# A fourth output buffer, and final DMA waits moved in front of the last store, in a fused dilated-window attention and GEGLU kernel

## Chip, cores, metric

One core of a Trainium2 chip. The metric is the device time of one launch in microseconds (us), the median of several runs. Runs agree within about 0.5%, and this case is about tenths of a microsecond in 195, so most of the argument rests on traces, which resolve 0.01 us.

## The reference

Two branches on the layer-normed input, and a residual; 2048 rows of 512, bf16.

```python
def _A_ref(x, wqkv, wo):            # 32 heads of 16; window of 8 keys, 2 apart
    qkv = (x @ wqkv) ...
    kg = k[:, :, idx_c, :]...; vg = v[:, :, idx_c, :]...
    logits = einsum("bhsd,bhswd->bhsw", q, kg) * scale   # masked before position 0
    return einsum("bhsw,bhswd->bhsd", softmax(logits), vg)... @ wo
def _B_ref(x, w_gate, w_up, w_down):
    return (gelu(x @ w_gate) * (x @ w_up)) @ w_down      # 1376 hidden columns
xn = _layernorm(x)
return x + _A_ref(xn, A_wqkv, A_wo) + _B_ref(xn, B_w_gate, B_w_up, B_w_down)
```

## The kernel before

The program builds a graph of tasks and orders it with a list scheduler at build time; each engine then runs its list, and semaphores carry the dependencies. Buffers are slots of pools: a task that starts a new tile takes the slot that came free first, and then depends on everything that used it. The output is made in 19 pieces. TensorE sums attention output and down projection in PSUM, VectorE adds the residual XR into an output buffer OB, and SyncE stores it. The last 256 rows are cut into 256- and 128-column pieces to shorten the end.

```python
TAIL_SPLIT = {14: [(0, 256), (256, 512)], 15: [(0, 256), (256, 384), (384, 512)]}
NOB = cfg.get("NOB", 3)                       # output buffers
P_ob = Pool("ob", NOB)
junk = sb("junk", [128, 512], BF)             # scratch: the sums of one tile want an output
# ... per piece:
it_ob = Item("ob" + sfx, P_ob, "ob")
#   fin (VectorE):  OB[:, slot, 0:CW] = PS[...] + XR[:, slot, c0:c1]
#   sto (SyncE):    dma_start(out2[rows, c0:c1], OB[:, slot, 0:CW])
```

Every DMA task gets one of 24 semaphores in turn. A task's waits stand in front of it, and SyncE ends with a wait for the full count of all 24:

```python
def emit_engine(self, eng_name, e):
    ...
    for t in self.order[eng_name]:
        for (s, v) in t.waits:
            e.wait_ge(s, v)
        ins = t.emit(e)
        ins.then_inc(t.sem, 16 if eng_name == "sp" else 1)
    if eng_name == "sp":
        for (s, tot) in self.dma_totals:      # 24 of them
            e.wait_ge(s, tot)
```

## Time and profile before

| | us |
|---|---|
| time, median of the first 3 runs | 194.91 (194.59 to 194.97) |
| span of the profiled execution | 192.8 |
| last matmul ends (modelled) | 190.32 |
| last add (VectorE) | 190.44 to 190.73 |
| last store issued | 190.76 |
| last store landed | 192.21 |
| SyncE's branch to the end | 192.39 |

The first half of such a reading is where the span is bound (TensorE, 97%); the second is the **tail**, from the end of the last matmul to SyncE's branch: 192.39 - 190.32 = 2.07 us here. As long as the build-time order stays as it is, a change of buffers and final waits can act nowhere else. The prediction below shows the lines. In them PE, DVE, ACT, POOL and SP are TensorE, VectorE, ScalarE, GpSimd and SyncE, PEld is TensorE's weight load, and a q behind an engine marks its instruction sequencer; numbers in front are start and duration in us, and brackets give the idle time before an instruction and who ended it. A store is issued by a SyncE instruction and has landed, or is home, when its data is written and its semaphore counted; a wait is met when its semaphore already has the value.

### The profile page before, as it was taken

What the parts mean: (1) busy time and instruction counts of PE and PEld (TensorE: products, weight loads), DVE (VectorE), ACT (ScalarE), POOL (GpSimd) and SP (SyncE); (2) the same over time, 40 slices, a digit from 0 to 9 for tenths busy, and PEclk for the clock granted to TensorE, in tenths of its full rate; (3) what the DMA queues carried; (4) which work ended last, traced back from release to release, by engine and by line L of the source; (5) the groups of instructions that cost most, each with busy time, mean ns of one, the idle gap of its engine ahead of it and who ended that gap; (6) DMA issues with size and microseconds to landing.
All of it is one profiled execution on the core that took longest, in us unless ns stands there. A gap on an engine that the chain in (4) does not pass through costs nothing.

```text
span 192.8 us, 3283 instructions
## 1 busy us (share of the span) xinstructions
PE 186.6 (97%) x1239; PEld 92.0 (48%) x1256; DVE 152.4 (79%) x240; ACT 106.1 (55%) x177; POOL 15.7 (8%) x31
## 2 busy tenths in 40 slices
PE   6899999999999999999999999999999999999994
PEld 2794444444444444444444444444444444444484
DVE  5799999999997965999995599998996199912132
ACT  5688565696896766712466587328276720058000
POOL 7010011110931020000000000000000000000000
PEclk9999999999999999999999999999999999999999
DMA  4999997899564014965401596420250496130121
GB/s 143 353 397 332 307 172 139 229 235 219 146 131 106 0 40 134 239 140 161 146 19 28 143 237 157 130 77 0 69 139 13 113 233 165 36 112 0 51 72 46
DMA packets 34800, 27.04 MB, mean 140 GB/s; under 512 B 11264, under 2 KB 33248, under 8 KB 34784
## 3 DMA queue, kind: packets, MB, share of 16 engines
q1 hardware_dynamic: 34784, 26.83, 56.2%
q8 instruction: 10, 0.16, 0.3%
q14 instruction: 6, 0.05, 0.1%
HBM read 19.99 MB, written 5.26 MB: 131 GB/s over the span
## 4 chain that ended last, share of the span: by engine, by line
PE 93%; DMA 4%; issue 1%; SPq 0%; DVE 0%; DVEq 0%
PE PS L1395 36%; PE PS L1474 18%; PE PS L1152 18%; PE PS L1470 7%; PE PS L1098 4%; PE PS L1363 4%; PE PS L1236 4%; DMA Wqkv<-in_A_wqkv_dram 2%; PE PS L1430 2%; DMA out_dram<-OB 1%; PE PS L1229 1%; SPq L923 0%; DVE OB L1494 0%; PE PS L1040 0%; DVEq L558 0%
## 5 line engine op out<-in xcount | busy, mean ns | idle before, releaser
L1412 ACT ACTIVATE UU<-PS 128x512 bf16<-128x512 f32 x40 | 24.1, 603 | 35.7 <-PE PS L1395 35.7
L1474 PE MATMUL PS<-Wd,HT 128*128 128x512 bf16 (+2 forms) x207 | 41.1, 345 | 0.1
L1395 PE MATMUL PS<-xnT,Wu 128*128 128x512 bf16 x155 | 39.8, 379 | 0.7 <-issue 0.5
L1395 PE MATMUL PS<-xnT,Wg 128*128 128x512 bf16 x155 | 39.2, 379 | 0.5 <-ACT OT L1375 0.2
L1206 DVE TENSOR_TENSOR UNI<-QT,KT 128x2048 bf16<-128x2048 bf16 x32 | 37.0, 1219 | 2.6 <-PE PS L1363 2.5
L1152 PE MATMUL PS<-xnT,Wqkv 128*128 128x512 bf16 x156 | 35.3, 379 | 0.2
L1417 DVE TENSOR_TENSOR HT<-GG,UU 128x512 bf16<-128x512 bf16 x40 | 16.6, 419 | 20.1 <-ACT UU L1412 20.0
L1405 ACT ACTIVATE GG<-PS 128x512 bf16<-128x512 f32 x40 | 23.7, 601 | 15.0 <-PE PS L1395 12.2
L1474 PEld LDWEIGHTS PS<-Wd,HT 128*128 128x128 bf16 x209 | 19.6, 98 | 18.6
L1395 PEld LDWEIGHTS PS<-xnT,Wu 128*128 128x128 bf16 x160 | 15.3, 98 | 19.6 <-issue 1.3
L1395 PEld LDWEIGHTS PS<-xnT,Wg 128*128 128x128 bf16 x160 | 15.5, 98 | 19.3 <-ACT OT L1375 0.4
L1152 PEld LDWEIGHTS PS<-xnT,Wqkv 128*128 128x128 bf16 x160 | 15.6, 98 | 18.6
L1343 DVE TENSOR_TENSOR BS<-BS,PT 128x2048 bf16<-128x2048 bf16 x16 | 19.6, 1224 | 0.4
L1343 DVE TENSOR_TENSOR UNI<-BS,PT 128x2048 bf16<-128x2048 bf16 x16 | 19.5, 1218 | 0.0
L1494 DVE TENSOR_TENSOR OB<-PS,XR 128x512 bf16<-128x512 f32 (+2 forms) x19 | 11.2, 603 | 10.0 <-PE PS L1474 9.4
L1470 PE MATMUL PS<-Wo,OT 128*128 128x512 bf16 (+2 forms) x76 | 16.9, 345 | 0.0
L1176 ACT ACTIVATE VT<-PS 128x512 bf16<-128x512 f32 x16 | 9.6, 597 | 4.4 <-PE PS L1152 4.4
L1375 ACT ACTIVATE OT<-PS 128x512 bf16<-128x512 f32 x16 | 8.3, 602 | 5.0 <-PE PS L1363 5.0
L940 DVE BATCH_NORM_STATS2 st<-XIN 128x6 f32<-128x512 bf16 x15 | 10.1, 686 | 0.9 <-DMA XIN<-in_A_x_dram 0.9
L1470 PEld LDWEIGHTS PS<-Wo,OT 128*128 128x128 bf16 x76 | 7.2, 98 | 7.0
L1192 POOL COPY KT<-KT 128x64 bf16<-128x64 bf16 x3 | 8.0, 2655 | 17.5 <-ACT KT L1169 16.1
L1162 ACT ACTIVATE QT<-PS 128x512 bf16<-128x512 f32 x12 | 7.2, 597 | 3.1 <-PE PS L1152 3.1
(73 smaller groups left out, 151.9 us busy)
## 6 DMA issues: line engine op xcount, KB each, us to landing
BS<-vt_scratch SPq DMA_DIRECT2D x64, 128.5 KB, 3.5
vt_scratch<-VT SPq DMA_DIRECT2D x16, 128.0 KB
XR<-in_A_x_dram SPq DMA_DIRECT2D x16, 128.0 KB, 2.2
out_dram<-OB SPq DMA_DIRECT2D x14, 128.0 KB, 1.9
Wqkv<-in_A_wqkv_dram SPq DMA_DIRECT2D x3, 512.0 KB
XIN<-in_A_x_dram SPq DMA_DIRECT2D x6, 256.0 KB, 4.4
Wg<-in_B_w_gate_dram SPq DMA_DIRECT2D x1, 1280.0 KB
Wu<-in_B_w_up_dram SPq DMA_DIRECT2D x1, 1280.0 KB
```

Of the source, the lines that this page charges most:

```text
L940: return lambda e: e.bn_stats(out=st[:, t, :], in_=XIN[:, it.slot, t2, :])
L1152: ins = e.matmul(PS[:, 512 * it.slot:512 * it.slot + HWD], lhsT=lhsT, rhs=xnT[:, itx.slot, kt, c0:c0 + HWD], start=(kt == 0), stop=(kt == 3))
L1176: return lambda e: e.activation(out=VT[:, ito.slot, 0:HWD], in_=PS[:, 512 * it.slot:512 * it.slot + HWD], func=ACTF.Identity)
L1206: return lambda e: e.tensor_tensor(out=UNI[:, it.slot, :, :], in0=bass.AP(QT, (itq.slot * 4 + g) * 512, [[NQT * 4 * 512, 128], [0, 4], [1, ...
L1343: return lambda e: e.tensor_tensor(out=dst(), in0=bass.AP(BS, it.slot * 4 * 514 + o, [[NBS * 4 * 514, 128], [514, 4], [128, 4], [1, 128]]) ...
L1395: ins = e.matmul(PS[0:M, 512 * it.slot:512 * it.slot + 512], lhsT=Wx[:, kt, j * 128:j * 128 + M], rhs=xnT[:, itx.slot, kt, :], start=(kt = ...
L1405: return lambda e: e.activation(out=GG[0:M, ito.slot, :], in_=PS[0:M, 512 * it.slot:512 * it.slot + 512], func=ACTF.Gelu_apprx_tanh)
L1412: return lambda e: e.activation(out=UU[0:M, ito.slot, :], in_=PS[0:M, 512 * it.slot:512 * it.slot + 512], func=ACTF.Identity)
L1417: return lambda e: e.tensor_tensor(out=HT[0:M, ito.slot, j, :], in0=GG[0:M, ig.slot, :], in1=UU[0:M, iu.slot, :], op=ALU.mult)
L1470: ins = e.matmul(PS[:, 512 * it.slot:512 * it.slot + CW], lhsT=OT[:, ito.slot, dq, ti * 128:(ti + 1) * 128], rhs=Wo[:, dq, c0:c1], start=( ...
L1474: ins = e.matmul(PS[:, 512 * it.slot:512 * it.slot + CW], lhsT=HT[:, ith.slot, j, ti * 128:(ti + 1) * 128], rhs=Wd[:, j, c0:c1], start=Fal ...
L1494: return lambda e: e.tensor_tensor(out=OB[:, ito.slot, 0:CW], in0=PS[:, 512 * it.slot:512 * it.slot + CW], in1=XR[:, itx.slot, c0:c1], op= ...
```

## The change

The intent: the last add should not wait for a buffer that an earlier store still reads (fourth buffer; its kilobyte per partition comes from the scratch tile, whose job XR's first buffer takes while it is still unused), and SyncE should not work through 24 waits at the very end, when 19 of them were met long before.

```diff
             for (s, v) in t.waits:
                 e.wait_ge(s, v)
+            if eng_name == "sp" and t is self.order["sp"][-1]:
+                late = self.order["sp"][-5:]
+                for (s, tot) in self.dma_totals:
+                    if not any(q.sem is s for q in late):
+                        e.wait_ge(s, tot)
             ins = t.emit(e)
@@
         if eng_name == "sp":
-            for (s, tot) in self.dma_totals:
-                e.wait_ge(s, tot)
+            for q in self.order["sp"][-5:]:
+                e.wait_ge(q.sem, q.val)
@@
-    NOB = cfg.get("NOB", 3)
+    NOB = cfg.get("NOB", 4)
@@
-        junk = sb("junk", [128, 512], BF)
@@
-  ("sx1",  ... dict(out=junk[:, :],  func=ACTF.Identity, accum_out=sums[:, 0:1]), ...
+  ("sx1",  ... dict(out=XR[:, 0, :], func=ACTF.Identity, accum_out=sums[:, 0:1]), ...
-  ("sxx1", ... dict(out=junk[:, :],  func=ACTF.Square, bias=sums[:, 1:2], ...
+  ("sxx1", ... dict(out=XR[:, 0, :], func=ACTF.Square, bias=sums[:, 1:2], ...
```

More of the change, by code (lines that the diff above doesn't have):

```diff
@@ L942, in bass_parallel_sum__sliding_local_dilated__glu_gated_geglu__prompt_kernel @@
                     for (nm, dur, kw, rd, wr) in (
-                            ("sx1", 0.55, dict(out=junk[:, :], func=ACTF.Identity, accum_out=sums[:, 0:1]),
+                            ("sx1", 0.55, dict(out=XR[:, 0, :], func=ACTF.Identity, accum_out=sums[:, 0:1]),
                              [], [I_junk, (I_sums, 0)]),
@@ L946, in bass_parallel_sum__sliding_local_dilated__glu_gated_geglu__prompt_kernel @@
                                                 scale=-1.0 / D), [(I_sums, 0)], [(I_sums, 1)]),
-                            ("sxx1", 0.55, dict(out=junk[:, :], func=ACTF.Square, bias=sums[:, 1:2],
+                            ("sxx1", 0.55, dict(out=XR[:, 0, :], func=ACTF.Square, bias=sums[:, 1:2],
                                                 accum_out=sums[:, 2:3]), [(I_sums, 1)], [I_junk, (I_sums, 2)]),
```

## The prediction

> **What bounds the kernel now.** I read the page first: busy time by engine, then the chain that ended last. TensorE is busy 97% of the span at full clock, and the chain runs through it for 93% of the span. Whatever does not shorten TensorE's stream can only act in the tail behind its last matmul, where the chain goes to the output adds (L1494) and the stores of OB (L1501).
>
> ```profile
> PE 186.6 (97%) x1239; PEld 92.0 (48%) x1256; DVE 152.4 (79%) x240; ACT 106.1 (55%) x177; POOL 15.7 (8%) x31
> PE 93%; DMA 4%; issue 1%; SPq 0%; DVE 0%; DVEq 0%
> ```
>
> The waits view restricted to tile OB says who holds the 19 output adds: TensorE nearly always, a store that still owns its buffer once. That once is the last add.
>
> ```profile
>   PE PS L1474: 9.4, 7
>   DMA out_dram<-OB: 0.6, 1
> DMA to landing us min/median/max: 1.7/2.0/2.9
> ```
>
> The chain of waits in order of time shows it: with three buffers the nineteenth add takes the buffer of the sixteenth, whose store was issued at 187.56, landed 2.85 us later (the slowest of all; the median is 2.0), and released the last add at 190.44.
>
> ```profile
> 187.11 0.44 DVE OB L1494
> 187.56 2.85 DMA out_dram<-OB
> 190.41 0.02 issue
> 190.44 0.29 DVE OB L1494
> ```
>
> So 0.56 us of idle time is booked on the missing buffer. The timeline of the same stretch shows whether the add could have started earlier.
>
> ```profile
> 188.70 0.78 PE L1474 MATMUL PS<-Wd,HT 128*128 128x128 bf16 x11
> 189.54 0.78 PE L1474 MATMUL PS<-Wd,HT 128*128 128x128 bf16 x11
> 189.59 0.29 DVE L1494 TENSOR_TENSOR OB<-PS,XR 128x128 bf16<-128x128 f32 x1 [0.38 <-PE PS L1474]
> 190.44 0.29 DVE L1494 TENSOR_TENSOR OB<-PS,XR 128x128 bf16<-128x128 f32 x1 [0.56 <-DMA out_dram<-OB]
> ```
>
> The next-to-last piece's matmuls end at 188.70 + 0.78 = 189.48 and its add, released by TensorE, starts at 189.59: 0.11 us later. The four adds before it start 0.11 to 0.14 us after theirs (same timeline, same subtraction). The last matmuls end at 189.54 + 0.78 = 190.32, so the last add would start at 190.43 to 190.46 with a free buffer; it did start at 190.44. **Matmul and store release it together.** The wait is real but hides nothing.
>
> Behind the last add: the timeline of the DMA issues has the last store issued at 190.76, and the semaphore instructions of the final waits (L564) follow it.
>
> ```profile
> L564 SPq EVENT_SEMAPHORE  x12: 17/28/539, 191.1 to 192.3; - x12
> ```
>
> In windows of 0.01 us the twelve start 0.06 us apart (191.20, 191.27, 191.33, ... 191.69). The tenth lasts 539 ns, until 192.23: it is the one that waits for the last store. Two follow, at 192.27 and 192.33, then the branch to the end at 192.39. The first nine lie under the store's flight and cost nothing.
>
> **What the Trainium skill says.** Perfetto Trace Analysis, Identifying Dependency Chains: an instruction with several waits may have EventSemaphore instructions inserted ahead of it. The trace agrees: 24 final waits are 12 such instructions (two waits each, the first single, one wait on the branch). Advanced Engine Details and Errata, Network/Comms: reading a semaphore from a sequencer takes 50 to 100 ns; here the pitch is 60 ns for an instruction with two waits. DMA: Bandwidth & Descriptors, Anatomy of one DMA: some 2 us of fixed cost, mostly the receipt of the write (stated there for the GpSimd path); the stores here take 1.7 to 2.9 us from SyncE, and that is the term that neither part of this change touches. Perfetto Trace Analysis, Optimization Strategy: a bubble that repeats can mean too few buffers. On OB it does not repeat: one in nineteen.
>
> **The change part by part.**
>
> Fourth buffer. The last add now takes the buffer of the fifteenth, whose store went out at about 185.96 and at the slowest landing of 2.9 us is home by 188.9, 1.5 us before it is wanted. Gain: 190.44 minus 190.43, so 0.00 to 0.02 us. Nowhere else does an add wait for a store, so nothing before the tail moves.
>
> Scratch. The two ScalarE sums write 128x512 into XR's first buffer and not into their own tile: same instructions, 631 and 722 ns, same order. The first load of XR is issued at 33.2 us, long after the sums (about 5 us), and ScalarE's later work already stands in front of it. 0.00 us.
>
> Order of instructions. The order on each engine is fixed at build time by a list scheduler that counts OB buffers, so a fourth one could reorder everything. I went through the plan of the kernel before: of 19 adds only the fourth was planned to wait for its buffer (by some half a microsecond), and VectorE has planned slack behind it; the visible effect should be that one store changes place with one XR load near 94 us. No planned time enters the forecast. 0.00 us expected.
>
> Final waits. 24 waits become 19 in front of the last store and 5 behind it. In the kernel before as compiled, the first-emitted of several waits sits on the instruction itself and the others go into semaphore instructions ahead of it. For the last store the first-emitted is the wait for the last add, so the 19 others become 10 semaphore instructions ahead of that wait, in time where SyncE idles. How much idle time? The store before is issued at 189.89 and takes 0.33, until 190.23; the last add is done at 190.44 + 0.29 = 190.73. Idle: 0.50 us. Needed: from the end of a store issue to the first semaphore instruction 0.055, nine pitches of 0.06, and 0.06 to what follows: 0.655 us. The last store is issued at 190.23 + 0.655 = 190.88 rather than 190.76: **0.12 us lost**. Its flight (190.76 to 192.23, 1.47 us) is the same. All 19 are met by then; the youngest is an earlier tile's store.
> After the landing, the five last waits are two semaphore instructions and the branch; by the same rule the last store's wait sits in the second of them, so only the branch follows. Two instructions of 0.06 us fall away behind the landing: **0.12 us gained**.
> Sum: -0.01 +0.00 +0.12 -0.12 = -0.01 us, nothing. Since SyncE is now later than the last add, even the buffer's 0.01 is covered. 194.91 - 0.01 = 194.9.
>
> **Rivals.** (1) The buffer's 0.56 us counts in full, as the waits view books it: 194.4. Against it: the matmul's end plus the usual lag falls on the same moment. For it: matmul ends are modelled, and in executions where the reused store lands later the buffer protects; then part of it appears. (2) The 10 semaphore instructions stand behind the wait for the add, as the source text orders them: 0.6 lost and 0.12 gained, 195.4. Against it: every several-wait instruction of the kernel before is compiled the other way round. (3) They are fully hidden, because the sequencer runs them faster than in the tail of before: only the 0.12 is left, 194.8. (4) The build-time order drifts after all: plus or minus 1 us, as TensorE's stream has gaps of about 6 us in total that could grow or shrink; no direction.
>
> **Range and chances.** The three runs before spread by 0.38 us, more than any tail term alone. Rivals 1 and 2 set the ends at 194.4 and 195.4; I trim the upper one slightly, as the compiled rule speaks against it. A change over 2% is 3.9 us, more than the whole tail behind the last matmul (192.8 - 190.32 = 2.5 us); only the reordering could do it, and I give that 1% each way.
>
> **What would show it.** Right: no wait of an add on an OB store in the waits view; the last add still 0.11 to 0.14 after the last matmul; ten semaphore instructions between the last two store issues at 0.06 pitch; the last store issued 0.1 to 0.15 us after the end of the last add; the branch about 0.04 after the landing; TensorE's count and busy time unchanged. Wrong: a last add clearly earlier against the last matmul, semaphore instructions that start only after the last add, or another order of matmuls.

## The result, and the profile after

194.75 us (194.39 to 195.04, 6 runs) against 194.78 us (194.42 to 194.97, 6 runs): ratio 1.000, 95% interval 0.9984 to 1.0015. A ratio here is the mean time of one kernel's fast runs over that of the other's of the same rounds, so not quite the ratio of the medians. The interval is 0.3 us to each side: the time says "the same", and nothing finer.

The page after: busy time by engine and chain that ended last.

```profile
PE 187.6 (97%) x1239; PEld 92.6 (48%) x1256; DVE 152.4 (79%) x240; ACT 106.1 (55%) x177; POOL 15.7 (8%) x31
PE 97%; issue 1%; DVE 0%; DVEq 0%
```

The counts are the same, and the DMA has left the chain. VectorE's, ScalarE's and GpSimd's busy times are the same to the tenth; TensorE's 1.0 us more is not the change's doing: it lies in front of the 101st matmul of the record (10.02 us busy there against 9.03), and behind it the work takes the same time, as follows. The chain in order of time, before and then after, has one piece that serves as a mark:

```profile
14.52 2.54 PE PS L1152 x11
```

```profile
14.88 2.54 PE PS L1156 x11
```

From this mark to the end of the last matmul it is 190.32 - 14.52 = 175.80 us before and 190.68 - 14.88 = 175.80 us after. The 0.4 us by which the span is longer lies in front of the mark. By the records of the traces the 101st matmul starts between 11.05 and 11.61 us, from execution to execution and in no order of kernels, and from there to the end of the last matmul it is 179.08 us in every profile but the one whose TensorE stream was changed. So the start makes noise, the body is constant, and the tail is what the change can move.

The waits on tile OB, the timeline of the last add, and the semaphore instructions in front of and behind the last store, all after:

```profile
  PE PS L1478: 9.9, 8
DMA to landing us min/median/max: 1.7/2.0/3.3
```

```profile
189.90 0.78 PE L1478 MATMUL PS<-Wd,HT 128*128 128x128 bf16 x11
190.78 0.29 DVE L1498 TENSOR_TENSOR OB<-PS,XR 128x128 bf16<-128x128 f32 x1 [0.55 <-PE PS L1478]
```

```profile
L563 SPq EVENT_SEMAPHORE  x10: 17/28/28, 190.6 to 191.2; - x10
L569 SPq EVENT_SEMAPHORE  x2: 28/28/28, 191.7 to 192.7; - x2
```

No add waits for a store, and the last add starts 190.78 - 190.68 = 0.10 us after the last matmul. Ten semaphore instructions stand between the last two store issues, and two behind the last. In numbers from the records:

| us | before | after |
|---|---|---|
| last matmul to last add | 0.12 | 0.11 |
| end of last add to issue of last store | 0.03 | 0.19 |
| issue of last store to branch | 1.63 | 1.54 |
| **tail**, last matmul to branch | **2.07** | **2.13** |

By these two looks the change lost 0.05 us. The other looks below show that this is not the whole story.

Going through the build-time orders of both kernels confirms that nothing else moved: the lists of TensorE, ScalarE, VectorE and GpSimd are identical, and in SyncE's one store and one XR load near 94 us have changed places.

### The profile page after: what moved, and what is told of

Read it like the earlier page. It is cut to its first block, busy times and chain, and to the rows that moved or that the text cites. A ratio compares the mean times of both kernels' runs of the same rounds, so it can differ in the third digit from the quotient of the medians.

```text
span 193.2 us, 3285 instructions
## 1 busy us (share of the span) xinstructions
PE 187.6 (97%) x1239; PEld 92.6 (48%) x1256; DVE 152.4 (79%) x240; ACT 106.1 (55%) x177; POOL 15.7 (8%) x31
## 4 chain that ended last, share of the span: by engine, by line
PE 97%; issue 1%; DVE 0%; DVEq 0%
PE PS L1399 36%; PE PS L1478 20%; PE PS L1156 18%; PE PS L1474 7%; PE PS L1102 4%; PE PS L1367 4%; PE PS L1240 4%; PE PS L870 2%; PE PS L1434 2%; PE PS L1233 1%; PE PS L1044 1%; DVE OB L1498 0%; DVE wsrc L819 0%; DVE Wd L843 0%; DVEq L558 0%
```

## The experiments

**Theory:** the three pieces are each small (buffer nothing, waits in front a loss of a little over 0.1 us, waits behind a gain of 0.1). **Rival:** they are large and cancel (buffer 0.5 us gained, waits 0.5 us lost). The time cannot tell them apart, since both say 194.8; parts done alone can. Only the buffer, only the waits, the waits further forward and two buffers ran on one chip; the add's wait first, five times and 76 more on a second; the two looks and the two late stores on a third; the moved fetch on a fourth. Every time is compared with runs of the kernel before on the same chip. Tails are collected in a table at the end of this part.

### Only the buffer

The change without its waits: the five lines in front of the last store out, the 24 waits behind it back.

```diff
-            if eng_name == "sp" and t is self.order["sp"][-1]: ...
-            for q in self.order["sp"][-5:]:
-                e.wait_ge(q.sem, q.val)
+            for (s, tot) in self.dma_totals:
+                e.wait_ge(s, tot)
```

> Only the fourth buffer and the scratch in XR; the 24 final waits stay behind the last store. Theory (buffer wait hidden by the matmul): last add 0.10 to 0.14 us after the last matmul's end, last store issued 0.03 us after the end of the last add, branch 1.63 us after that issue, all as before; time -0.02 us, ratio 1.000 within 0.002. Rival (the two parts cancel: buffer gains 0.5 us, moved waits lose it): 0.5 us faster, ratio 0.9975.

194.42 us against 194.59; ratio 0.9984 (0.9963 to 1.0005). Tail 2.06 us: add 0.11 after the matmul, store 0.03 after the add, branch 1.63 after the store, all as foretold. The 0.5 us of the rival's ratio (0.9975) is inside the interval too, however; the profile speaks for the theory, the time does not decide.

### Only the waits

```diff
-    NOB = cfg.get("NOB", 4)
+    NOB = cfg.get("NOB", 3)
```

> Only the moved waits (and the scratch in XR), three buffers. Theory: ten semaphore instructions between the last two store issues, which stand 0.66 us apart from end to start; last store issued 0.15 to 0.20 us after the last add, branch 1.53 us after that issue; net +0.05 to +0.1 us, ratio 1.000 within 0.002. Rival (the two parts cancel): 0.5 us slower, ratio 1.0025.

194.66 us against 194.59; ratio 0.9993 (0.9970 to 1.0016); the rival's 1.0025 is outside. Tail 2.12 us: store 0.19 after the add, branch 1.53 after the store. The moved waits cost their 0.16 and give back 0.10, whether there are three or four buffers.

### The waits further forward

SyncE idles 1.3 us in front of the third-last store. The 19 waits fit there whole; and with the last store's wait emitted first, it is compiled onto the branch itself.

```diff
-            if eng_name == "sp" and t is self.order["sp"][-1]:
+            if eng_name == "sp" and t is self.order["sp"][-3]:
@@
-            for q in self.order["sp"][-5:]:
+            for q in reversed(self.order["sp"][-5:]):
```

> The change, but the 19 waits stand in front of the third-last store, where SyncE idles 1.3 us for an add, and of the five last waits the last store's is emitted first, so that it sits on the branch. Theory: last store issued 0.03 us after the last add, branch 1.48 to 1.50 us after that issue (1.63 before, 1.53 with the change): 0.15 us faster than before, 0.2 faster than the change, ratio about 0.9992, hardly to be told from 1 in the time but plain in the trace. Rival (moved waits cost nothing wherever they stand): same as the change, last store 0.20 us behind the last add.

The semaphore instructions of this kernel, moved and final:

```profile
L563 SPq EVENT_SEMAPHORE  x10: 17/28/28, 188.0 to 188.5; - x10
L569 SPq EVENT_SEMAPHORE  x2: 28/114/201, 191.1 to 191.2; - x2
```

The ten are over at 188.5, the two final ones lie under the store's flight, and the branch waits for the landing alone. Store 0.03 us after the add, branch 1.46 after the store, tail 1.88 us: 0.24 us shorter than the change's. Time 194.35 us against 194.59; ratio 0.9980 (0.9959 to 1.0001), so not clear of 1.

### The place of the add's wait in the compiled list

```diff
+            fw = tots[:10] + t.waits + tots[10:]     # for the last store only
-            for (s, v) in t.waits:
+            for (s, v) in fw:
                 e.wait_ge(s, v)
```

> The change with the waits of the last store emitted so that the wait for the last add is compiled into the first of the ten semaphore instructions and not onto the store: what the source text seems to say. Theory: the nine others run after the add, at 0.06 us each, so the last store is issued 0.6 us after the end of the last add (0.20 with the change); 0.4 us slower than the change, ratio to before about 1.002. Rival (the place in the compiled list does not matter): same as the change.

Store 0.64 us after the end of the add, tail 2.58 us, 0.45 longer than the change's: **the place in the list is worth 0.45 us**, although the source's loops look as if the waits were simply taken in turn. But the time was 195.14 us against 195.38, ratio 0.9994 (0.9974 to 1.0014), where 1.002 was expected. The trace agreed with the theory to 0.05 us and the time missed by about 0.5 us, to the side of "before is slower than thought".

### Five times as many waits in front, and 76 more behind

```diff
-                for (s, tot) in self.dma_totals: ...  e.wait_ge(s, tot)
+                for k in range(5):
+                    for (s, tot) in self.dma_totals: ...  e.wait_ge(s, tot - k)
```

> The change with each of the 19 front waits repeated five times: 48 semaphore instructions in front of the last store instead of 10. All are met at once. Theory: 38 more at 0.06 us, none of them hidden, since the ten already fill SyncE's idle time: last two store issues 2.93 us apart from end to start, 2.3 us slower, ratio 1.0115. Rival (waits in front are hidden behind the matmul and the add): 0.5 us slower at most, ratio 1.002.

For the other kernel the final waits become 81, with those of the five last stores in the middle of the list, so that the last store's is compiled into the first instruction:

```diff
-            for q in self.order["sp"][-5:]:
-                e.wait_ge(q.sem, q.val)
+            more = [(s, tot - k) for k in range(1, 5) for (s, tot) in ...]    # the other 19
+            for (s, v) in more[:36] + [(q.sem, q.val) for q in late] + more[36:]:
+                e.wait_ge(s, v)
```

> The change with 76 more waits, all met, behind the last store, and the last store's own wait in the first of the 40 semaphore instructions, so that 39 follow the landing. Theory: each costs 0.06 us after the landing as in front of the issue: branch at 1.53 + 2.34 = 3.87 us after the last issue, 2.3 us slower, ratio 1.012. Rival (waits behind the last store run under its flight and cost nothing): ratio 1.000.

The semaphore instructions in front of the last store of the first, and behind that of the second:

```profile
L564 SPq EVENT_SEMAPHORE  x48: 17/28/28, 190.5 to 193.3; - x48
```

```profile
L572 SPq EVENT_SEMAPHORE  x40: 27/28/1094, 191.7 to 195.1; - x40
```

Both rivals fall. The last two store issues stand 2.96 us apart (0.67 with the change), so 38 more instructions cost 2.30 us; behind the store, 38 more put the branch at 3.87 us after the issue (1.54), 2.33 us for the 39 that follow the landing. **Each semaphore instruction of two met waits costs 60 ns on either side**, and is free only under something else. The times were 197.00 and 197.13 us against 195.38, ratios 1.0085 (1.0063 to 1.0107) and 1.0093 (1.0075 to 1.0112): 1.65 and 1.8 us slower than before where 2.3 was expected. Again the trace agreed to 0.03 us, and again the kernel before seemed half a microsecond slower than its profile.

### Two buffers

```diff
-    NOB = cfg.get("NOB", 3)
+    NOB = cfg.get("NOB", 2)
```

> The kernel before with two output buffers: does a missing buffer show where it must? The build-time order differs only in the tail (the adds of the last two pieces change places) and by one store near 94 us. Theory: the last add must wait for the landing of the 256-column store issued at 189.2 in the profile of before, 1.9 to 2.9 us later, so it starts at 191.1 to 192.1 instead of 190.44: 0.7 to 1.7 us slower, ratio 1.0035 to 1.009; the waits view shows 1 us or more of adds behind stores. Rival (output buffers never matter here): ratio 1.000.

195.20 us against 194.59; ratio 1.0027 (1.0002 to 1.0052), slower; the expected range of 1.0035 to 1.009 begins inside this interval. Who held the adds, in the view of tile OB:

```profile
  PE PS L1474: 9.0, 6
  DMA out_dram<-OB: 1.6, 1
```

The tail is 2.88 us. But the store that held them was not the one I had named: that one (issued at 189.18) was home at 190.86. It was the store issued at 187.51, home at 190.70 after 3.19 us; its add started at 190.72, and the last add, behind it on VectorE, at 190.94. This is the very store that the kernel before waits for. Why is it, at 64 KB, slower than the 128 KB stores with their 2.0?

### Two more looks at the kernel before, and a late store on purpose

> The kernel before, another look: how far does the landing of the reused store vary, and does the last add follow it? Theory: lag of the last add behind the last matmul is 0.11 us if the store lands within 2.85 us, and the landing's excess over that otherwise (0.4 us at 3.3). My prediction's step (the buffer is worth 0.00 to 0.02 us) would need a lag of 0.11 to 0.13 here too.

> The kernel before, a third look, for the same question and with the same numbers as the second.

The chain in order of time and the timeline of the second look, then the chain of the third:

```profile
187.53 3.40 DMA out_dram<-OB
190.93 0.02 issue
190.95 0.29 DVE OB L1494
```

```profile
189.50 0.78 PE L1474 MATMUL PS<-Wd,HT 128*128 128x128 bf16 x11
190.95 0.29 DVE L1494 TENSOR_TENSOR OB<-PS,XR 128x128 bf16<-128x128 f32 x1 [1.11 <-DMA out_dram<-OB]
```

```profile
187.84 3.44 DMA out_dram<-OB
191.28 0.02 issue
191.30 0.29 DVE OB L1494
```

**The first profile was a lucky one.** Here the store took 3.4 us, and the last add started 0.67 and 0.71 us after the last matmul, 0.57 and 0.60 later than TensorE allowed. Tails 2.62 and 2.66 us. (Both looks are single runs, 195.15 and 195.37 us, of which only the traces are used.) This step of my prediction, the buffer at 0.00 to 0.02 us, fails; and this is the half microsecond that the times of the second chip asked for (the runs there are not profiled, so for them it is an inference).

To force the case, I put 36 met semaphore instructions in front of that store in SyncE's idle time, so that it is issued 1 us or more late, and ran this with three and with four buffers (and without waits in front of the last store).

```diff
-            if eng_name == "sp" and t is self.order["sp"][-1]:
+            if eng_name == "sp" and t is self.order["sp"][-4]:
+                late = self.order["sp"][-6:]      # then the other 18 waits, four times
@@
-    NOB = cfg.get("NOB", 4)
+    NOB = cfg.get("NOB", 3)                       # in the first of the two
```

> Three buffers, and the 256-column store whose buffer the last add takes is issued about 1 us late on purpose (36 met semaphore instructions in front of it, in time where SyncE idles; no waits in front of the last store, the last store's wait on the branch). In nine profiles so far this store took 2.6 to 3.3 us to land, and with three buffers the add can only be unheld if it takes under 2.9. Theory: the add starts at the landing, 2.6 to 3.3 us after an issue at 188.55, so 0.7 to 1.4 us late against the last matmul (0.11 normally); the tail is longer by as much than in the same kernel with four buffers, ratio to it about 1.005. Rival (a busy buffer never reaches the end): lag 0.11 us, no difference to four buffers.

> The same with four buffers. Theory: the last add takes an older buffer and starts 0.11 us after the last matmul although the store is late by 1 us; last store issued 0.03 us after the add, branch 1.46 us after that: tail from last matmul to branch 1.88 us, ratio to before about 0.999. Rival (the late store itself, not its buffer, sets the end): tail as long as with three buffers.

The chain of the one with three buffers:

```profile
189.01 1.53 DMA out_dram<-OB
190.54 0.02 issue
190.56 0.29 DVE OB L1499
```

The first expectation missed, and told the most. Issued at 189.01 and 188.81 and not at 187.5, **the same store lands in 1.53 us**, in both kernels. The last add is 0.14 us behind the matmul with three buffers and 0.11 with four; tails 1.92 and 1.89; 194.54 and 194.53 us against 194.92, ratios 0.9986 (0.9971 to 1.0002) and 0.9987 (0.9968 to 1.0005). A store made late on purpose came home hardly later than in the first look (190.54 against 190.41) and before those of the second and third. So the slowness belongs to the moment, not to the store.

### What the store meets

A store is counted home when its last share is: the Trainium skill, DMA: Bandwidth & Descriptors, Why a DMA increments its semaphore by 16 and not by 1, says that up to 16 DMA engines finish independently and the semaphore counts them. The traces agree: 16 increments for each store. In all eleven profiles in which this store goes out at its usual time, its fifteenth share is home 1.52 to 1.54 us after the issue, and the sixteenth 2.57 to 3.44 us after it. One DMA engine is late. The DMA view of the second look at the kernel before, for 188.9 to 190.0 us, when fifteen shares are home or nearly so, has almost nothing else:

```profile
DMA packets 5, 0.03 MB, mean 24 GB/s; under 512 B 0, under 2 KB 3, under 8 KB 3
q8 instruction: 1, 0.02, 5.4%
q14 instruction: 1, 0.01, 1.7%
q1 hardware_dynamic: 3, 0.00, 1.2%
```

A block of instructions (16 KB, from 188.93 to 189.88 by the packet records), another of 8 KB, and then three late packets of the store. The Trainium skill, Runtime: NRT & Kernel Launch, Instruction fetch mechanics, says that each engine's instructions are refilled by DMA in 16 KiB blocks of 256. The traces have records of 16 KB on q8, and on q14 of 8 KB. The page of the kernel before lists ten packets of that kind on q8; 10 x 256 = 2560 is about what 1256 matmuls and 1256 weight loads need (2512; four traces have all matmuls, the others lack 17 records), so by its count q8 is TensorE's stream (my estimate, from these numbers and that page). The records side by side:

| profile | 16 KB fetch ends | 16th share home | difference |
|---|---|---|---|
| before, first look | 189.36 | 190.41 | 1.05 |
| before, second look | 189.88 | 190.93 | 1.05 |
| before, third look | 190.23 | 191.28 | 1.05 |
| only the waits | 189.51 | 190.53 | 1.02 |
| two buffers | 189.59 | 190.70 | 1.11 |
| the change | 190.17 | 191.22 | 1.05 |
| only the buffer | 188.96 | 189.94 | 0.98 |
| the other four (early waits, add's wait first, five times, 76 more) | 189.45 to 190.01 | 190.50 to 191.06 | 1.05 to 1.06 |

The share comes home 1.0 to 1.1 us after the fetch, however late the fetch is. The 8 KB block does not fit: from its end to the share it is 1.09 us in the first look, 1.51 in the second and 3.06 with the change. The late store of the two kernels above was issued in the second half of the fetch (it ended at 189.19 and 189.18), and its packets came after it. The test of this reading is to move the fetch and leave the store alone: 64 more instructions in TensorE's stream, far ahead of the tail, in the kernel before.

```diff
+            if eng_name == "pe" and t is self.order["pe"][110]:
+                dv, ac = ...                   # the last VectorE and ScalarE tasks of 20 us earlier
+                for k in range(64):            # 64 instructions of two met waits each
+                    e.wait_ge(dv.sem, dv.val - k)
+                    e.wait_ge(ac.sem, ac.val - k)
```

> The kernel before, three buffers, with 64 semaphore instructions (all waits met) put into TensorE's stream near 105 us, so that its later instruction fetches fall 64 instructions earlier in the work; the last 16 KB fetch should then end near 186 and not, as in eleven profiles, between 189.0 and 190.2, over the flight of the store whose buffer the last add takes. Theory (in those eleven profiles that store's 16th share lands 1.0 to 1.1 us after the fetch's end, its other fifteen within 1.6 us of the issue: one share waits behind the fetch): here all 16 shares land within 1.6 us, the last add starts 0.11 us after the last matmul, tail to the branch 2.06 us. Rival (the store is slow for another reason, its own size or its place in the queue): 16th share still 2.6 to 3.4 us after the issue. The body may grow by up to 3 us for the 64 instructions, so the time itself is no test.

The DMA views of two stretches, the fetch at its new place and then the whole flight of the store, and the timeline of the last add:

```profile
q8 instruction: 1, 0.02, 5.7%
```

```profile
DMA packets 172, 0.08 MB, mean 47 GB/s; under 512 B 25, under 2 KB 172, under 8 KB 172
q1 hardware_dynamic: 172, 0.08, 16.9%
out_dram<-OB SPq DMA_DIRECT2D x1, 64.0 KB, 1.5
```

```profile
195.17 0.29 DVE L1500 TENSOR_TENSOR OB<-PS,XR 128x128 bf16<-128x128 f32 x1 [0.55 <-PE PS L1480]
```

The fetch now ends at 190.70, 4.4 us before the end of the last matmul (195.06) where it used to end 0.4 to 1.2 us before. The 8 KB block on q14 kept its place (start 1.1 us before that end, 1.2 to 1.3 in the three looks), so it is q8 that carries TensorE's stream. All 16 shares are home 1.53 us after the issue; the last add is released by TensorE with three buffers, 0.11 us behind it; the tail is 2.06. The body pays 4.7 us for the 64 instructions (183.77 for 179.08), so the time, 199.17 against 194.98 us, ratio 1.0215 (1.0194 to 1.0236), is a by-product, and larger than the 3 us I had allowed. It is one look against eleven, but with nothing of the store changed.

The same trace holds a second test, in other stores. The store that goes out at 127.23 in the kernel before meets a fetch (127.08 to 128.00); with the fetches moved, it goes out at 131.98 and meets none. The one at 184.95 meets none before; moved, at 189.70, it meets the fetch that ends at 190.70. SyncE's instruction for each (line and duration in ns), the kernel before and then the fetches moved:

```profile
L1501 SPq DMA_DIRECT2D out_dram<-OB x1: 1137/1137/1137, 127.2 to 127.2; - x1
L1501 SPq DMA_DIRECT2D out_dram<-OB x1: 436/436/436, 185.0 to 185.0; - x1
```

```profile
L1507 SPq DMA_DIRECT2D out_dram<-OB x1: 431/431/431, 132.0 to 132.0; - x1
L1507 SPq DMA_DIRECT2D out_dram<-OB x1: 1379/1379/1379, 189.7 to 189.7; - x1
```

The first is home after 1.98 us and no longer 2.53, the second after 2.78 and no longer 2.12. Here it is not one share that is late: the issue itself lasts until 0.37 us after the fetch's end, in both, and all sixteen shares come late. So the fetch holds up the stores that it meets, and the hold-up moves with it. Which DMA engine the fetch used the trace does not say; that it is the late share's is inferred from the fixed distance and from these interventions.

### The tails side by side

| kernel | buffers | matmul to add | add's end to store | store to branch | tail |
|---|---|---|---|---|---|
| before, three looks | 3 | 0.12, 0.67, 0.71 | 0.03 | 1.63 | 2.07, 2.62, 2.66 |
| the change | 4 | 0.11 | 0.19 | 1.54 | 2.13 |
| only the buffer | 4 | 0.11 | 0.03 | 1.63 | 2.06 |
| only the waits | 3 | 0.11 | 0.19 | 1.53 | 2.12 |
| waits further forward | 4 | 0.11 | 0.03 | 1.46 | **1.88** |
| add's wait first | 4 | 0.11 | 0.64 | 1.54 | 2.58 |
| five times in front | 4 | 0.11 | 2.78 | 1.53 | 4.71 |
| 76 more behind | 4 | 0.11 | 0.19 | 3.87 | 4.46 |
| two buffers | 2 | 0.67 | 0.21 | 1.72 | 2.88 |
| late store, three | 3 | 0.14 | 0.03 | 1.46 | 1.92 |
| late store, four | 4 | 0.11 | 0.03 | 1.46 | 1.89 |
| fetch moved | 3 | 0.11 | 0.03 | 1.63 | 2.06 |

## Why the prediction was right, and where it was not

- **Total:** 194.9 forecast, 194.75 measured, "same". Right, with the caution that every kernel here without extra instructions would have been "same" at 2%: the interval of 0.3 us to each side could not have shown the wrong term below.
- **TensorE's body and the order:** unchanged, as forecast; one store and one load changed places near 94 us, as forecast.
- **Scratch in XR:** no trace of it. ScalarE's busy time is 106.1 us before and after.
- **Waits in front:** forecast 0.12 us lost; measured 0.19 - 0.03 = 0.16. The gap between the issues was 0.67 (forecast 0.655), and the issue of the store before it ended 0.48 and not 0.50 us ahead of the add's end (in the profile of before, too, that store was issued at 189.91, where I had read 189.89). Right mechanism, size a quarter too small. That the add's wait sits on the store itself is what keeps it this small: 0.64 us otherwise.
- **Waits behind:** forecast 0.12 us gained; measured 1.63 - 1.54 = 0.09 to 0.10. Right. (The flight I gave for the stores, 1.7 to 2.9 us, is that of the 5 of 19 for which the view gives a landing; by the records the 32 KB ones at the end take 1.45.)
- **The buffer: wrong.** The prediction's step was "0.00 to 0.02 us", from one profile in which store and matmul released the add within 0.02 us of each other. I read this coincidence as a property. In the other two looks the buffer would have been worth 0.57 and 0.60 us. Over the eleven profiles in which the store goes out at its usual time, the landing comes after the moment at which TensorE would release the last add by 0.3 to 0.6 us in six and by less than 0.1 in five; mean of the excess 0.26 us (my arithmetic from the records: landing against the end of the last matmul plus 0.085, the usual lag of 0.11 less the 0.025 from landing to add; in the profiles with four buffers nothing waited for it). My first rival named the protection in other executions and gave it no weight in the middle estimate.
- **What the change is worth, then:** against the lucky tail of before it loses 0.05 us, against the other two it gains 2.62 - 2.13 = 0.5. On average some 0.2 us or 0.1% by the traces, below what the times can show: 1.000 with 0.0015 to each side. The rival that two half-microseconds cancel is refuted for the waits and half true for the buffer: a gain of up to 0.6 us exists in some executions, and the waits take back only 0.06 of it.
- **Best version:** the waits further forward with four buffers has the shortest tail, 1.88 us. Its time is 0.9980 of before (0.9959 to 1.0001). I call that likely faster than both, not shown.

What stays open: whether the fetch's moment differs by chip or only by execution (it ended between 188.96 and 190.23 in eleven profiles), and why the half microsecond shows in the times of the second chip and not in those of the first comparison.

## What to carry to other kernels

Read a wait that ends together with another in more than one profile before calling it harmless: its ends may drift apart by more than all the terms of the estimate, and the time of a landing is set by the slowest of its shares. A semaphore instruction of met waits cost SyncE 60 ns wherever nothing covered it; put such waits where SyncE idles for something else, and give the last wait to the instruction that must follow it. Against differences of 0.1%, split the span into start, body and tail: here the start varied by 0.56 us and the body not at all.

## What the Trainium skill lacked or had wrong

- Runtime: NRT & Kernel Launch, Instruction fetch mechanics, tells how instructions are fetched and why the engine does not wait for them, but no page says what a fetch costs the DMA traffic beside it: with a 16 KB fetch in its way a 64 KB store landed in 2.57 to 3.44 us, without it in 1.53, and two stores issued during a fetch kept SyncE for 1.14 and 1.38 us where 0.43 and 0.44 were usual.
- DMA: Bandwidth & Descriptors, Anatomy of one DMA, gives some 2 us of fixed cost for the GpSimd path; SyncE's 32 KB stores at the end took 1.44 to 1.55 us from issue to landing.
- Perfetto Trace Analysis, Identifying Dependency Chains, says that several waits become semaphore instructions ahead of the instruction, but not which wait goes where: the first emitted sits on the instruction and the rest go ahead of it, and moving one wait from there into the first semaphore instruction cost 0.45 us.
- Advanced Engine Details and Errata, Network/Comms, has 50 to 100 ns for reading a semaphore; a met semaphore instruction with two waits costs SyncE 60 ns (48 of them in a row), which no page gives.
